# One order of side work for another in a fused attention and two-MLP kernel: where a weight's split, the steps of three batches' attention and a few late casts stand

## The chip, the cores and the metric

The kernel runs on one core of one Trainium2 chip. The metric is the device time of one execution in microseconds (us), the median of a few runs.

## The reference

Three computations follow each other. Inputs are drawn in float64 for the weights; the result is float32.

```python
x = attention(q, k, v)            # 4 batches, 8 heads, 576 tokens, 64 dims
                                  # heads 0-3: a window of 32; heads 4-7: every 32nd token
x = x.transpose(0, 2, 1, 3).reshape(2304, 512)
x = ((x @ w_a) * (x @ w_b)) @ w_out      # 512 -> 1536 -> 512
h = x @ w_in                             # 512 -> 2048
x = (h * (1 / (1 + exp(-h)))) @ w_out2   # 2048 -> 512
```

## The kernel before

**Numbers.** Every matmul operand is split in two: a high part, cast on ScalarE (ACT), and a low part, the difference, on VectorE (DVE). TensorE (PE) multiplies high by high, high by low and low by high: three passes. A weight arrives as pairs of int32 words of a float64 and has to be made float32 first, in five steps: ACT makes the exponent's rest (merge step 0, L670) and a rebased copy of the high word (L652), DVE joins them in two steps (merge 1, L673, then merge 2, L678, which reads what merge 1 wrote), and GpSimd's queue (POOL) stores the result in DRAM for later groups (L691). Then `split_w` makes the two parts, ACT's cast L698 and DVE's subtraction L699, two blocks ahead of the matmuls that use them.

**Order.** Tokens go through in five groups of 512 (the last has 256). Groups 0 and 1 run through the gated MLP (phases A0, blocks 0 to 35, and A1, 36 to 71) and the second MLP (B0, 72 to 103, and B1, 104 to 135). A block is 12 matmuls of PE, an "up" product (L706) or a "down" product (L1381 in phase A, L1401 in phase B), 2.72 us at full clock. Everything else is written by hand into the blocks: after a block's matmuls have been issued, `block(p)` runs the steps of one of two strings, the first for p below 36, the second from there on. Its letters are: 0, 1, 2 the merge steps; B the rebased copy; Y the split of the weight for block p+2; K the store to DRAM; W the loads; N, R, M, X, O a batch's attention: normalise (DVE L490, L497, POOL L503), prepare (DVE transposes L277 of q and k, scaled copies L387), mask and maximum (DVE L455, L464), softmax (ACT, one exp a segment, L478), and store of the attention's result as x (ACT L591, DVE L594). Nothing is reordered afterwards: each engine does its list in this order. Merges stand in every block from 3 to 32, and in two of three blocks from 34 to 89.

**Attention in blocks.** Batch 0 is done ahead of block 0; batches 1 to 3 are spread over the blocks by `PLAN`, which gives the block at which the batch's loads and transposes begin, the first block of each of four groups of units (two, three, two and two units), and the end of the next batch's loads. `plan_attention` sets the rest at fixed distances: scores (PE L441) at the end of block first+1, masks and exps one unit a block from first+2, normalise one block later, the transposes of probabilities (PE L523) and products with v (PE L563) later, and the store. A group's scores go into a bank of PSUM (`att`, two buffers), and the next user of the bank waits until the store has read it. Within a batch the units of the first two groups are of local heads (type 0), the other groups strided (type 1). Transposes of q and k stand one a block: of type 0 in the four blocks from the batch's start, of type 1 in four blocks that end in front of the third group.

**End of phase A.** In blocks 35 and 71 the accumulators of the gated MLP are taken out as the split y (ACT L1391, DVE L1392), which the second MLP's blocks read.

**Late stage.** From about 491 us to the end groups 2 and 3 go through as sums of seven products (up products L986, down products L1047), group 4 between them. ACT copies a product's result to `u` (L997), a DVE step joins them (L1001), then silu (ACT L1027, DVE L1029) and the split of its result (ACT L716, DVE L717). Here the order is written by the time that a table of 2.72 us per block gives each event (`ready`): the split is put where its event is due.

Of the kernel before, what the change touches and what calls it, by code (L numbers as in the profile page):

```python
# [85 lines left out]
MM, MM_HALF, BLOCK = 0.2267, 0.12, 2.72  # L86
# [8 lines left out]

PLAN = {
    1: (0, [2, 10, 19, 27], 36),
    2: (37, [41, 49, 58, 66], 79),
    3: (80, [82, 89, 97, 105], 0),
}  # L100

TOGETHER = ((0, 1), (2, 3, 4), (5, 6), (7, 8))

PAIR_OF = (2, 3)

STEPS = ("NRM0BK1O2YXW", "N0O1B2MKWYRX")

NEG = -1.0e9
REBASE = 2.0 ** -112
# [4 lines left out]
def attention_gated_mlp_silu_mlp(  # L114
# [610 lines left out]
    def plan_attention(batch, s0, first, end):  # L725

        add = lambda at, place, f, *a: plan.setdefault((at, place), []).append((f, a))

        def spread(loads, n, s0, s1):
            for m in range(n):  # L730
                add(s0 + m * (s1 - s0) // n, "load", next, loads, None)

        starts = {us[0]: s for us, s in zip(TOGETHER, first)}
        first1 = starts[NL]
        turn1 = first1 - 2
        for one in range(4):
            add(s0 + (one if batch.b > 1 else one // 2), "prepare", batch.transpose_qk, 0, one)
            add(turn1 - 4 + one, "prepare", batch.transpose_qk, 1, one)
        spread(batch.load_qk(1), 9, s0 + (4 if batch.b > 1 else 2), turn1 - 7)
        spread(batch.load_vs(), 4 * TAKE + 5, s0 + 4 * (batch.b > 1), first1 + 3)  # L740
        for us, s in zip(TOGETHER, first):
            others = len(us) - 1
            add(s + 2, "tensor", batch.scores, *us)
            for n, u in enumerate(us):
                add(s + n - others, "prepare", batch.prepare, u)
                add(s + n + 2, "mask", batch.mask, u)
                add(s + n + 2, "mask", batch.largest, u)
                add(s + n + 2, "softmax", batch.softmax, u)
                add(s + n + 3, "normalise", batch.guard, u)
                add(s + n + 3, "normalise", batch.normalise, u)  # L750
                add(s + others + 6, "turned", batch.turned, u)
                add(s + others + 7, "store", batch.store, u)
            add(s + others + 6, "tensor", batch.turn, *us)
            add(s + others + 7, "tensor", batch.values, *us)
        after = Batch(batch.b + 1, False)
        if after.b < B:
            spread(after.load_qk(0), 9, turn1 + 2, end)
            spread(after.load_vl(), 10, first1 + 7, end)
        return after
# [6 lines left out]
    def block(p):  # L766
# [5 lines left out]
        c = conv_at.get(p)  # L772
        for step in STEPS[p >= NA]:
            if step == "K":
# [16 lines left out]
    with tc.manual_schedule():  # L791
# [11 lines left out]
        batch = Batch(0, 7)  # L803
# [39 lines left out]
        for s in range(-1, max(nu + LV, max(PART), max(CONV) + 1) + 1):  # L843
# [7 lines left out]
            for step in ORDER:  # L851
# [13 lines left out]
                elif step == "A" and s in PART:  # L865
                    i = PART[s]
# [17 lines left out]
        batch = after  # L884
# [10 lines left out]
        def at(t, f, *a):  # L895
            events.append((t, len(events), f, a))
# [7 lines left out]
        def products(f, n, cost, ws=(), h=None):  # L904

            t = clock[0]
            at(t, f)
            clock[0] = t + n * cost
            for key in ws:
                used.setdefault(key, [t, t])[1] = clock[0]  # L910
            if h is not None:
                held.setdefault(h, [t, t, None])[1] = clock[0]
            return clock[0]
# [121 lines left out]
        ready = {}  # L1035
# [15 lines left out]
        def twin(n, kinds, js, half_n, fillers, places):  # L1051

            chains = [Chain(n, kind, j, c) for c, (kind, j) in enumerate(zip(kinds, js))]
            fillers = list(fillers)
            m = 0
            for s in CHAIN_ORDER:
                for chain in chains:
                    end = products(lambda s=s, chain=chain: chain.multiply(s), 6, MM, [chain.key(s)])
                    at(end, chain.evacuate, s)
                    quad = QUADS.get(s)  # L1060
                    if quad is not None and (chain.c or chain.kind == "i"):
                        j = chain.j + half_n * quad[1]
                        f, a = (gated, (chains, quad)) if chain.kind == "b" else (silu, (chain, quad))
                        if quad[0]:
                            at(end, f, *a, j)
                        else:
                            key = (chain.kind, 2, j)
                            at(end, keep_act, key, f, *a, None)
                            ready[key] = end
                    m += 1  # L1070
                    for _ in range(places.get(m, 0)):
                        if fillers:
                            products(*fillers.pop(0))
            for filler in fillers:
                products(*filler)
# [34 lines left out]
        for f in range(H1):  # L1110
            twin(("o", f), "ab", (f, f), H1, down_o(f - 1) if f else (), {10: 2})
# [14 lines left out]
        for j in range(N1):  # L1126
            key = ("b", 3, j)
# [85 lines left out]
        for f in range(0, H2, 2):  # L1213
            if f:
                twin(("p", f), "ii", (f, f + 1), H2, down_p(f - 2 + H2) + down_p(f), dict.fromkeys(range(1, 15), 1))
            else:
                last_o = [down_of("o", "b", N1 - 1, d, N1) for d in range(CC)]
                twin(("p", f), "ii", (f, f + 1), H2, last_o + down_p(f), {1: CC, **dict.fromkeys(range(9, 15), 1)})
# [4 lines left out]
        for j in range(N2):  # L1223
            key = ("i", 3, j)
# [70 lines left out]
        for key in in_order:  # L1295
# [4 lines left out]
            elif key[0] == "B":  # L1300
                n, c = key[1:]
                kind, j = ("ab"[c], n[1]) if n[0] == "o" else ("i", n[1] + c)
                needs((kind, j), (n, c, 0), t)
            elif key[0] == "B22":
                for c in range(2):
                    n = key[1]
                    kind, j = ("ab"[c], n[1] + H1) if n[0] == "o" else ("i", n[1] + c + H2)
                    needs((kind, j), (n, c, 1), t)
            elif key[0] == "T12":
                n, c = key[1:]  # L1310
# [30 lines left out]
        for ph, g in PHASES:  # L1341
# [7 lines left out]
            for kind, j in half[ph]:  # L1349
                if batch.b < B and p == PLAN[batch.b][0]:  # L1350
                    batch = plan_attention(batch, *PLAN[batch.b])
# [111 lines left out]
```

## Time and profile before

| | us |
|---|---|
| median of 3 runs (lowest to highest) | 944.64 (941.54 to 947.15) |
| the profiled execution | 944.54 |
| span of its trace | 942.7 |
| PE busy in it | 920.4 (98%) |
| DVE busy | 665.6 (71%) |
| ACT busy | 541.3 (57%) |
| POOL busy | 82.3 (9%) |
| mean granted clock of PE | 0.989 |

The span is the traced part of the execution; 1.8 us lie around it. PE is busy nearly throughout, so what can be won is the time in which it stands still, and the time in which it works at the lower clock. The waits of PE by cause, and the stretch in which they lie, are the views to read; the other engines' busy shares are means over stages that differ.

### The profile page before, as it was taken

What the parts mean: (1) busy time and instruction counts of PE and PEld (TensorE: products, weight loads), DVE (VectorE), ACT (ScalarE), POOL (GpSimd) and SP (SyncE); (2) the same over time, 40 slices, a digit from 0 to 9 for tenths busy, and PEclk for the clock granted to TensorE, in tenths of its full rate; (3) what the DMA queues carried; (4) which work ended last, traced back from release to release, by engine and by line L of the source; (5) the groups of instructions that cost most, each with busy time, mean ns of one, the idle gap of its engine ahead of it and who ended that gap; (6) DMA issues with size and microseconds to landing.
All of it is one profiled execution on the core that took longest, in us unless ns stands there. A gap on an engine that the chain in (4) does not pass through costs nothing.

```text
span 942.7 us, 15848 instructions
## 1 busy us (share of the span) xinstructions
PE 920.4 (98%) x5626; PEld 748.3 (79%) x5626; DVE 665.6 (71%) x1248; ACT 541.3 (57%) x1274; POOL 82.3 (9%) x139
## 2 busy tenths in 40 slices
PE   9999899999999989999999999999999999999998
PEld 5767678787778778778888888888999788878897
DVE  5588888776777767666777666665587776766475
ACT  3558778666667566565543444345575554554474
POOL 2232222111111111100000000000000000000000
PEclk9799999999999999999999999999999999999999
DMA  9999789898888995333242222223464121225361
GB/s 168 196 280 276 230 250 277 255 241 251 254 232 237 272 219 179 108 86 97 92 116 75 67 67 67 57 72 120 123 184 141 45 83 58 83 67 168 119 207 45
DMA packets 163647, 145.29 MB, mean 154 GB/s; under 512 B 96800, under 2 KB 119904, under 8 KB 163568
## 3 DMA queue, kind: packets, MB, share of 16 engines
q1 hardware_dynamic: 154758, 121.81, 48.1%
q0 software_dynamic: 6720, 21.63, 6.9%
q10 hardware_dynamic: 2090, 0.84, 0.4%
q8 instruction: 44, 0.72, 0.3%
q14 instruction: 35, 0.29, 0.1%
HBM read 121.70 MB, written 22.54 MB: 153 GB/s over the span
## 4 chain that ended last, share of the span: by engine, by line
PE 71%; DVE 12%; ACT 7%; issue 4%; DMA 4%; POOL 0%; SPq 0%; DVEq 0%; ACTq 0%; POOLq 0%
PE ring L706 15%; PE ring L986 12%; PE att L986 8%; PE acc L1047 8%; PE acc L1401 6%; PE acc L1173 4%; PE att L1047 4%; PE ring L1047 4%; PE acc L706 3%; ACT prs L478 2%; DVE raw L673 2%; DVE raw L678 2%; DVE w L699 2%; PE acc L1381 1%; ACT raw L670 1%
## 5 line engine op out<-in xcount | busy, mean ns | idle before, releaser
L706 PE MATMUL ring<-x,w 128*128 128x512 f32 (+1 forms) x816 | 168.3, 358 | 6.7 <-DVE w L699 5.6
L706 PEld LDWEIGHTS ring<-x,w 128*128 128x128 f32 x816 | 133.6, 191 | 33.3 <-DVE w L699 10.2
L1277 DVE TENSOR_TENSOR w<-raw,w 128x512 fp32r<-128x512 f32 (+1 forms) x164 | 106.2, 655 | 29.5 <-ACT w L1276 26.7
L1276 ACT CAST w<-raw 128x512 fp32r<-128x512 f32 (+1 forms) x164 | 95.7, 592 | 20.8 <-PE att L1047 11.0
L699 DVE TENSOR_TENSOR w<-raw,w 128x512 fp32r<-128x512 f32 x136 | 93.1, 692 | 3.7 <-ACT w L698 2.7
L706 PE MATMUL ring<-y,w 128*128 128x512 f32 x384 | 94.0, 394 | 0.0
L1401 PE MATMUL acc<-w,h 128*128 128x512 f32 x384 | 93.3, 392 | 0.6 <-DVE w L699 0.4
L698 ACT CAST w<-raw 128x512 fp32r<-128x512 f32 x136 | 82.5, 619 | 4.0 <-DVE raw L678 4.0
L1401 PEld LDWEIGHTS acc<-w,h 128*128 128x128 f32 x384 | 71.3, 188 | 17.0 <-DVE w L699 1.6
L706 PEld LDWEIGHTS ring<-y,w 128*128 128x128 f32 x384 | 71.8, 189 | 15.6 <-DVE w L699 0.6
L716 ACT CAST h<-h 128x512 fp32r<-128x512 f32 (+1 forms) x48 | 27.2, 567 | 86.8 <-DVE h L1022 41.0
L1381 PE MATMUL acc<-h,w 128*128 128x512 f32 x288 | 72.2, 397 | 3.5 <-DVE w L699 2.0
L1381 PEld LDWEIGHTS acc<-h,w 128*128 128x128 f32 x288 | 52.8, 188 | 18.1 <-DVE w L699 4.0
L717 DVE TENSOR_TENSOR h<-g,h 128x512 fp32r<-128x512 f32 (+1 forms) x64 | 39.9, 624 | 31.6 <-ACT h L716 31.4
L986 PE MATMUL ring<-operands,w 128*128 128x512 f32 x240 | 61.3, 398 | 0.0
L716 ACT CAST h<-g 128x512 fp32r<-128x512 f32 (+1 forms) x64 | 36.3, 567 | 42.4 <-DVE g L1373 30.4
L986 PE MATMUL ring<-x,w 128*128 128x512 f32 x240 | 59.5, 391 | 1.2 <-ACT u L997 1.2
L986 PE MATMUL att<-operands,w 128*128 128x512 f32 x240 | 60.4, 395 | 0.0
L478 ACT ACTIVATE prs<-sm,nm 128x54 f32<-128x54 f32 (+1 forms) x120 | 39.7, 333 | 30.0 <-DVE nm L464 29.7
L673 DVE SCALAR_TENSOR_TENSOR raw<-words,raw 128x512 int32<-128x512 int32 x68 | 47.7, 702 | 10.7 <-ACT raw L670 10.0
L986 PEld LDWEIGHTS ring<-operands,w 128*128 128x128 f32 x240 | 44.9, 188 | 11.7 <-DVE w L1277 1.1
L678 DVE SCALAR_TENSOR_TENSOR raw<-e,raw 128x512 int32<-128x512 int32 x68 | 48.8, 718 | 7.5 <-ACT e L652 0.7
(200 smaller groups left out, 1559.8 us busy)
## 6 DMA issues: line engine op xcount, KB each, us to landing
raw<-keptp SPq DMA_DIRECT2D x80, 256.0 KB
raw<-kepti SPq DMA_DIRECT2D x64, 256.0 KB
words<-in_moe_w_out_dram SPq DMA_DIRECT2D x28, 512.0 KB
raw<-kepto SPq DMA_DIRECT2D x48, 256.0 KB
raw<-kepta SPq DMA_DIRECT2D x36, 256.0 KB
raw<-keptb SPq DMA_DIRECT2D x36, 256.0 KB
words<-in_moe_w_in_dram SPq DMA_DIRECT2D x16, 512.0 KB
words<-in_moe_w_a_dram SPq DMA_DIRECT2D x12, 512.0 KB
```

Source lines behind the costliest of these rows:

```text
L673: nc.vector.scalar_tensor_tensor(out=z, in0=high, scalar=SIGN, in1=z, op0=ALU.bitwise_and, op1=ALU.bitwise_or)
L678: nc.vector.scalar_tensor_tensor(out=z, in0=rebased.pop(c), scalar=3, in1=z, op0=ALU.logical_shift_left, op1=ALU.bitwise_or)
L698: nc.scalar.copy(out=o[:, 0], in_=t)
L699: nc.vector.tensor_tensor(out=o[:, 1], in0=t, in1=o[:, 0].bitcast(F32), op=ALU.subtract)
L706: nc.tensor.matmul(ps[:, :T], lhsT=w[:, wi, c * P:(c + 1) * P], rhs=x[:, xi, c, :T], start=(c == 0 and wi == 0 and xi == 0), stop=(c == CC ...
L716: nc.scalar.copy(out=o[:, 0, :T], in_=t32[:, :T])
L986: nc.tensor.matmul(self.acc[acc], lhsT=w[:, wi, (2 * part + c) * P:(2 * part + c + 1) * P], rhs=x[:, xi, c], start=(begin and c == 0 and m ...
L1047: nc.tensor.matmul(accs[d], lhsT=lhsT, rhs=rhs, start=(first and wi == 0 and xi == 0), stop=(last and wi == 1))
L1276: nc.scalar.copy(out=o[:, 0, cols], in_=t)
L1277: nc.vector.tensor_tensor(out=o[:, 1, cols], in0=t, in1=o[:, 0, cols].bitcast(F32), op=ALU.subtract)
L1381: nc.tensor.matmul(accs[d], lhsT=w[:, wi, d * P:(d + 1) * P], rhs=h[:, xi], start=(j == 0 and wi == 0 and xi == 0), stop=(j == N1 - 1 and ...
L1401: nc.tensor.matmul(accs[t][:, :DM], lhsT=h[:, xi, t * P:(t + 1) * P], rhs=w[:, wi, :], start=(j == 0 and wi == 0 and xi == 0), stop=(j == ...
```

## The change

It consists of five edits. In the strings the split Y goes between merge 1 and merge 2 (on ACT ahead of B; from block 36 on also ahead of the mask M). Batches 2 and 3 get other first blocks in `PLAN`, and batch 3's start and the loads' ends move with them. The type-1 transposes stand one block later relative to their group. In `plan_attention` a unit's store is put a block later for the third unit of a group of three. In the late stage the split of the second MLP's silus made from the chain's product 2 is due one block later (16 such events).

```diff
--- before.py
+++ after.py
@@ -95,15 +95,15 @@
 
 PLAN = {
     1: (0, [2, 10, 19, 27], 36),
-    2: (37, [41, 49, 58, 66], 79),
-    3: (80, [82, 89, 97, 105], 0),
+    2: (37, [41, 49, 59, 68], 76),
+    3: (76, [79, 87, 97, 105], 0),
 }
 
 TOGETHER = ((0, 1), (2, 3, 4), (5, 6), (7, 8))
 
 PAIR_OF = (2, 3)
 
-STEPS = ("NRM0BK1O2YXW", "N0O1B2MKWYRX")
+STEPS = ("NRM0K1YBO2XW", "N0O1YB2MKWRX")
 
 NEG = -1.0e9
 REBASE = 2.0 ** -112
@@ -732,7 +732,7 @@
 
         starts = {us[0]: s for us, s in zip(TOGETHER, first)}
         first1 = starts[NL]
-        turn1 = first1 - 2
+        turn1 = first1 - 1
         for one in range(4):
             add(s0 + (one if batch.b > 1 else one // 2), "prepare", batch.transpose_qk, 0, one)
             add(turn1 - 4 + one, "prepare", batch.transpose_qk, 1, one)
@@ -749,7 +749,7 @@
                 add(s + n + 3, "normalise", batch.guard, u)
                 add(s + n + 3, "normalise", batch.normalise, u)
                 add(s + others + 6, "turned", batch.turned, u)
-                add(s + others + 7, "store", batch.store, u)
+                add(s + others + 7 + n // 2, "store", batch.store, u)
             add(s + others + 6, "tensor", batch.turn, *us)
             add(s + others + 7, "tensor", batch.values, *us)
         after = Batch(batch.b + 1, False)
@@ -1066,7 +1066,7 @@
                         else:
                             key = (chain.kind, 2, j)
                             at(end, keep_act, key, f, *a, None)
-                            ready[key] = end
+                            ready[key] = end + BLOCK * (chain.kind == "i" and s == 2)
                     m += 1
                     for _ in range(places.get(m, 0)):
                         if fillers:
```

On ACT, around block 20 of phase A0: `L591 COPY` is the store of the third unit of a group, which frees its PSUM bank (L1364 is the copy of a gate's product). Before:

```order
L670 ACTIVATE raw<-words 128x512
L652 ACTIVATE e<-words 128x512
L591 CAST x<-att 128x2x128
L591 CAST x<-att 128x2x64
L591 COPY x<-att 128x2x64 x2
L698 CAST w<-raw 128x512
L670 ACTIVATE raw<-words 128x512
L652 ACTIVATE e<-words 128x512
L698 CAST w<-raw 128x512
L1364 COPY a<-ring 128x512
```

After:

```order
L670 ACTIVATE raw<-words 128x512
L698 CAST w<-raw 128x512
L652 ACTIVATE e<-words 128x512
L591 CAST x<-att 128x2x128
L591 CAST x<-att 128x2x64
L591 COPY x<-att 128x2x64
L670 ACTIVATE raw<-words 128x512
L698 CAST w<-raw 128x512
L652 ACTIVATE e<-words 128x512
L591 COPY x<-att 128x2x64
L1364 COPY a<-ring 128x512
```

The third unit's copy moves behind the next block's three instructions (L670, L698, L652), and L698 goes ahead of L652 in each block.

On DVE, in blocks 70 and 71, at the end of phase A1 (L1392 is the low part of y). Before:

```order
L490 TENSOR_SCALAR su<-su 128x4
L497 RECIPROCAL rs<-su 128x4
L673 SCALAR_TENSOR_TENSOR raw<-words,raw 128x512
L678 SCALAR_TENSOR_TENSOR raw<-e,raw 128x512
L699 TENSOR_TENSOR w<-raw,w 128x512
L1392 TENSOR_TENSOR y<-acc_2299,y 128x512
L1392 TENSOR_TENSOR y<-acc_2300,y 128x512
L1392 TENSOR_TENSOR y<-acc_2301,y 128x512
L1392 TENSOR_TENSOR y<-acc_2302,y 128x512
L673 SCALAR_TENSOR_TENSOR raw<-words,raw 128x512
L678 SCALAR_TENSOR_TENSOR raw<-e,raw 128x512
```

After:

```order
L673 SCALAR_TENSOR_TENSOR raw<-words,raw 128x512
L699 TENSOR_TENSOR w<-raw,w 128x512
L678 SCALAR_TENSOR_TENSOR raw<-e,raw 128x512
L455 SCALAR_TENSOR_TENSOR sm<-att,mask_str 128x162 x2
L464 TENSOR_REDUCE nm<-sm 128x6
L1392 TENSOR_TENSOR y<-acc_2299,y 128x512
L1392 TENSOR_TENSOR y<-acc_2300,y 128x512
L1392 TENSOR_TENSOR y<-acc_2301,y 128x512
L1392 TENSOR_TENSOR y<-acc_2302,y 128x512
L490 TENSOR_SCALAR su<-su 128x6
L497 RECIPROCAL rs<-su 128x6
L673 SCALAR_TENSOR_TENSOR raw<-words,raw 128x512
```

A unit's mask and maximum (L455, L464) now stand ahead of y's evacuation, the guard and reciprocal (L490, L497) behind it, and each split L699 between L673 and L678.

On DVE, the last transposes of batch 3's first k (`kT`, before in blocks 82 and 83, now in 78 and 79). Before:

```order
L699 TENSOR_TENSOR w<-raw,w 128x512
L277 STREAM_TRANSPOSE kT<-kld 128x576
L1373 SCALAR_TENSOR_TENSOR g_4005<-th,ring 128x512
L717 TENSOR_TENSOR h<-g_4005,h 128x512
L699 TENSOR_TENSOR w<-raw,w 128x512
L277 STREAM_TRANSPOSE kT<-kld 128x576
L673 SCALAR_TENSOR_TENSOR raw<-words,raw 128x512
L678 SCALAR_TENSOR_TENSOR raw<-e,raw 128x512
L455 SCALAR_TENSOR_TENSOR sm<-att,mask_loc 128x128 x2
L464 TENSOR_REDUCE nm<-sm 128x4
```

After:

```order
L673 SCALAR_TENSOR_TENSOR raw<-words,raw 128x512
L699 TENSOR_TENSOR w<-raw,w 128x512
L678 SCALAR_TENSOR_TENSOR raw<-e,raw 128x512
L277 STREAM_TRANSPOSE kT<-kld 128x576
L673 SCALAR_TENSOR_TENSOR raw<-words,raw 128x512
L699 TENSOR_TENSOR w<-raw,w 128x512
L678 SCALAR_TENSOR_TENSOR raw<-e,raw 128x512
L1373 SCALAR_TENSOR_TENSOR g_3994<-th,ring 128x512
L717 TENSOR_TENSOR h<-g_3994,h 128x512
L699 TENSOR_TENSOR w<-raw,w 128x512
L455 SCALAR_TENSOR_TENSOR sm<-att,mask_loc 128x128 x2
L464 TENSOR_REDUCE nm<-sm 128x4
```

Before, the last transpose had two instructions between it and the first mask of those keys; now a merge with its split, a silu's two steps (L1373, L717) and another split stand between them.

## Rows read from the trace of the kernel before

**Rows 1.** Page, section 4: chain of waits that ended last, by engine

```profile
PE 71%; DVE 12%; ACT 7%; issue 4%; DMA 4%; POOL 0%; SPq 0%; DVEq 0%; ACTq 0%; POOLq 0%
```

**Rows 2.** Table by stretch: length, busy us per engine, PEclk, DMA share

```profile
56.00:178.00 122.00, 113.79 (x826) 88.79 (x824) 102.48 (x198) 90.80 (x234) 24.18 (x41) 0.99 0.96 262
...
178.00:293.00 115.00, 111.62 (x792) 88.35 (x793) 83.99 (x166) 75.77 (x203) 18.81 (x29) 1.00 0.87 246
...
293.00:436.00 143.00, 138.70 (x984) 112.10 (x983) 98.86 (x194) 88.17 (x232) 15.17 (x24) 0.99 0.62 173
```

**Rows 3.** Waits of PE, whole span: us in total, times, longest

```profile
PE ring L706 <- DVE w L699: 5.6, 7, 2.0
PE att L441 <- DVE kT L277: 5.1, 4, 2.9
PE acc L1381 <- DVE w L699: 2.0, 2, 1.4
PE ring L986 <- ACT u L997: 1.2, 1, 1.2
PE ring L706 <- ACT x L591: 1.0, 1, 1.0
```

**Rows 4.** Timeline, DVE in phase A0: start, us, engine, line, operation

```profile
92.20 0.69 DVE L673 SCALAR_TENSOR_TENSOR raw<-words,raw 128x512 int32<-128x512 int32 x1
...
92.99 0.69 DVE L678 SCALAR_TENSOR_TENSOR raw<-e,raw 128x512 int32<-128x512 int32 x1
...
93.60 0.69 DVE L699 TENSOR_TENSOR w<-raw,w 128x512 fp32r<-128x512 f32 x1
...
94.20 0.48 DVE L455 SCALAR_TENSOR_TENSOR sm<-att,mask_loc 128x128 f32<-128x128 f32 x2
...
95.06 0.68 DVE L673 SCALAR_TENSOR_TENSOR raw<-words,raw 128x512 int32<-128x512 int32 x1
```

**Rows 5.** Timeline around the end of block 20, ACT and PE

```profile
124.51 0.72 PE L441 MATMUL att<-kT,qs 64*64 64x54 f32 x20
124.64 0.74 ACT L670 ACTIVATE raw<-words 128x512 int32<-128x512 uint8 x1
```

**Rows 6.** Page, section 5: two groups of ACT, busy us, mean ns

```profile
L698 ACT CAST w<-raw 128x512 fp32r<-128x512 f32 x136 | 82.5, 619 | 4.0 <-DVE raw L678 4.0
...
L478 ACT ACTIVATE prs<-sm,nm 128x54 f32<-128x54 f32 (+1 forms) x120 | 39.7, 333 | 30.0 <-DVE nm L464 29.7
```

**Rows 7.** Timeline of the phase's end: evacuation of y, then the next matmuls

```profile
291.41 2.63 ACT L1391 CAST y<-acc 128x512 fp32r<-128x512 f32 x4 [0.42 <-PE acc L1381]
...
292.57 2.47 DVE L1392 TENSOR_TENSOR y<-acc,y 128x512 fp32r<-128x512 f32 x4
...
296.44 2.77 PE L706 MATMUL ring<-y,w 128*128 128x512 f32 x10
```

**Rows 8.** Timeline of the scores of batch 3's first group, DVE and PE

```profile
328.38 0.77 DVE L277 STREAM_TRANSPOSE kT<-kld 128x576 f32<-128x576 f32 x1
...
329.30 0.27 PE L441 MATMUL att<-kT,qT 64*32 64x64 f32 x2 [0.87 <-DVE kT L277]
...
331.62 0.77 DVE L277 STREAM_TRANSPOSE kT<-kld 128x576 f32<-128x576 f32 x1
...
332.44 1.96 PE L441 MATMUL att<-kT,qT 64*32 64x64 f32 x62 [2.88 <-DVE kT L277]
```

**Rows 9.** Table by stretch, as Rows 2, just after three waits of PE

```profile
103.40:107.40 4.00, 3.97 (x10) 3.16 (x11) 3.64 (x11) 3.24 (x10) 1.14 (x2) 0.57 0.70 210
...
236.60:239.00 2.40, 2.40 (x11) 1.98 (x12) 2.02 (x5) 1.17 (x4) 0.97 (x2) 1.00 0.92 351
...
332.40:336.00 3.60, 3.56 (x67) 3.11 (x68) 2.76 (x6) 0.66 (x4) 0.00 (x0) 0.55 0.96 191
```

**Rows 10.** Timeline, DVE idle behind a softmax of batch 3

```profile
391.60 0.69 DVE L1373 SCALAR_TENSOR_TENSOR g<-th,ring 128x512 f32<-128x512 f32 x1 [2.06 <-ACT th L1371]
```

**Rows 11.** Timeline, PE's longest wait for a split

```profile
103.43 2.85 PE L706 MATMUL ring<-x,w 128*128 128x512 f32 x6 [2.00 <-DVE w L699]
```

## The prediction, on record before the changed kernel ran

> **What bounds the kernel now.** I read first the chain of waits that ended last: the tensor engine (PE) holds 71% of it, VectorE (DVE) 12%, ScalarE (ACT) 7% [rows 1]. So time is won or lost where PE waits for one of those two, and nowhere else. Then the table by stretch says where it waits: PE stands idle 8.2 us of the 122 in phase A0, 3.4 of 115 in A1 and 4.3 of 143 in the phases B [rows 2]. DVE is busy for 102 of the first 122 us, against 84 of 115 and 99 of 143 afterwards: it sets the pace in A0, while later it has slack that is not evenly spread. Last, the waits of PE by cause [rows 3]: 5.6 us in seven waits for a weight's low part, 5.1 for the transposed keys, 2.0 in two waits for a low part in the down products, 1.2 for a copied `u` in the late stage, 1.0 for a stored x. These are what the change can take away; behind a long wait PE also works at a lower clock for some us (below).
>
> The sum is made against the profiled execution, 944.54 us, which is 0.1 under the median of the three runs. About 0.5%, 4.7 us, is what a measurement of this kernel can tell from no change.
>
> **The change, part by part.**
>
> *The split between the merges, phase A0.* Merge 2 reads what merge 1 wrote, and starts 0.79 us after it (92.20 to 92.99); the split behind it belongs to another weight and starts 0.61 after merge 2 [rows 4]. With the split between them all three can start 0.61 apart, so a block with a merge is 0.18 shorter on DVE. Up to block 20 that is 18 merges, 3.2 us at most, but there the moved store takes it back (next paragraph). From block 21 to 34 there are 13 merges: 13 x 0.18 = 2.3. I take **-2.3**; the bounds are 0 (DVE waits for ACT's merge step 0 in place of the old gap) and -5.2 (all 29 merges of blocks 3 to 32, without a toll at block 20).
>
> The Trainium skill, page "VectorE: DVE Perf Modes", section "The DRAIN you can't avoid", speaks against this term: the next DVE operation starts only when the pipe is empty, and "you cannot skip it by chaining ops without semaphores"; the section itself sends instructions that nothing holds to another section, where they may start earlier. By the first sentence the order of the three would not matter and the term would be 0. The rows do not agree with it: the two starts are 0.79 and 0.61 apart, the second less than the 0.69 that the instruction itself takes [rows 4].
>
> *The third unit's store a block later.* At block 20 the second scores product takes a PSUM bank when the third unit's copy has read it. Before, PE starts there at 124.51, and block 20's first ACT instruction follows at 124.64 [rows 5]. Now three of those (an exponent step, a cast, a rebased copy, each about 0.62 as the cast's mean [rows 6]) stand ahead of the copy: 3 x 0.62 = 1.9 us. PE comes to it that much too early, and the 3.2 us of the first 20 blocks end there. From block 36 on the same move has no scores close behind it. So nothing is added beyond the lost gain.
>
> *Block 36.* PE waits 1.0 us for x, which ACT stores at the change of phase [rows 3]. ACT's cast for the split now goes ahead of the store: 0.62 [rows 6]. **+0.6** (0 to +0.7).
>
> *Batch 2, blocks 41 to 66.* Masks now stand behind a split, 0.61 later, and the type-1 transposes and the last two groups one or two blocks later. The two waits in the down products, 2.0 together, lie here [rows 3]: they may shorten by 1.4 or grow by 0.61 each. **+0.4** (-1.4 to +1.2), near no change, since the number of operations is the same.
>
> *Blocks 70 and 71.* A mask with its six exps is put into block 70, in front of y's evacuation. The exps are 0.33 each, 2.0 together [rows 6]. Before, ACT began y's casts at 291.41, as the accumulators ended, and DVE ended the low parts at 292.57 + 2.47 = 295.04 [rows 7]. Now both are 2.0 later, 297.0, and behind them stand a guard, a reciprocal, a merge and the split for block 73, some 1.5 us: 298.5. PE wants it at 296.44 [rows 7], so it waits 2.1 there and up to 1.0 in block 74, whose split follows. **+2.6** (+2.0 to +3.1).
>
> *Keys of batch 3.* The last two transposes came 0.87 and 2.88 us too late, 3.75 together, and the scores and the block behind them ran at 0.55 of the clock for 3.6 us, which loses 1.6 [rows 8, 9]: 5.4. Now the last transpose stands a whole block, 2.72 us, further ahead of the scores. PE was there 0.87 + 0.27 + 2.88 = 4.0 before the last one was done, so 4.0 - 2.72 = 1.3 could be left; DVE's list in these blocks is a little shorter, so I take 0.7, too short a wait for the clock to fall. **-4.7** (-5.4 to -4.1).
>
> *Masks of batch 3.* Its groups begin three and two blocks earlier, where merges still run. A mask and its maximum take 0.86 (94.20 to 95.06 [rows 4]). The nearest row is a block that has a transpose beside its split: DVE went round in 3.24 us (328.38 to 331.62 [rows 8]) against PE's 2.72, so it loses 0.5 a block; with a mask as well 1.4. The first group has two such blocks, 81 and 82: +2.8 less what lead the splits have there; **+2.4** (+1.4 to +3.4, the last with the split's 0.61). Of the second group one mask falls on the last merge, block 89: 0 to 0.86 + 0.79 + 0.61 = 2.3, **+1.2**. In the last two groups masks stand 0.61 later, behind a split. DVE idles 2.06 us behind such a softmax [rows 10] because its next list waits for ACT, so a later mask is passed on: up to 0.61 for each of four units, 2.4; half of it, **+1.2**, since the splits have about that lead. Together +4.8.
>
> *Late silus.* The split's ACT cast goes behind the copy of `u` that PE waits 1.2 us for [rows 3]. **-1.2** (-1.2 to 0); the other fifteen casts have no wait of PE near them, and cost nothing while a block's lead remains.
>
> Sum: -2.3 + 0.6 + 0.4 + 2.6 - 4.7 + 4.8 - 1.2 = +0.2, so 944.54 + 0.2 = **944.7 us**.
>
> **The rivals.**
>
> *Slower: three new waits reach 2 us and the clock falls.* After a wait of 2.00 us the clock stood at 0.57 for 4.0 us, which costs 4.0 x 0.43 = 1.7 on top [rows 9, 11]; after one of 1.4 (the longest in the down products [rows 3]) it stayed at 1.00 [rows 9]. My sum puts waits of about that size at blocks 73 and 85 and a shorter one at 103. Where each comes out as one piece of 2.0 or more, it adds 3 x 1.7 = 5.1: 949.8. For it: the estimates at 73 and 85 are above 2. Against it: a loss can come as several short waits.
>
> *Faster: the splits' lead covers the masks.* DVE is idle 31 us of 115 in A1 and 44 of 143 in B [rows 2], and the number of masks is what it was. If the splits stand two blocks ahead by enough, the terms +2.6 and +4.8 are gone: 937.3. Against it: DVE already was late before at just such places, 5.6 and 2.0 us [rows 3].
>
> *The exchange of the merges gives nothing.* If the gap of 0.79 only moves, the term -2.3 is missing: 947.0.
>
> **How the numbers follow.** The forecast, waits removed about as large as waits made, has 0.40; the faster rival 0.30, since seven of its us rest on leads that I worked out by hand and not on a row; the slower one 0.21; the exchange without gain 0.09. Faster by over 0.5% is under 939.8: the faster rival and a little of the forecast's lower side, less the part of that rival that stops short, 0.32. Slower is above 949.3: the slower rival with some of the upper bounds, 0.22. The rest, 0.46, lies between. The range goes from 936, just below the faster rival, to 951.5, above the slower one by 1.7, one more fall of the clock.
>
> **What would show it.** In the changed profile: DVE's merge 1, split and merge 2 at 0.61 us steps; no wait for a low part between blocks 21 and 35, but one of some 2 us before the second scores product at block 20; the wait of the scores for keys under 1 us; a wait for the low part at blocks 73 and 85 of about 2 us each, and short ones at 103 and 111; no wait for `u` in the late stage. Wrong would be the whole account if PE's idle time fell in A0 by 5 us, or if no wait for a split appeared between 290 and 350 us; and the sum, if a clock of 0.55 showed behind more than one of them.

## The result, and the profile after

The changed kernel takes 955.93 us, the median of four runs (952.51 to 958.27); the kernel before beside it 944.86. The ratio is 1.0117 (1.0073 to 1.0161): **slower by 11 us**. The forecast was 944.7, with no change as the likeliest and 951.5 as the upper end. The profiled execution of the changed kernel is its shortest, 952.51, with a span of 950.7.

From 33 to 45 us of the profiled execution before, PE works at 0.50 of its clock; after, at 1.00. Both happen in executions of the other kernels below too, so the two traces are compared from block 5 on, by the start of each block's first matmul.

| start of | before | after | difference | since the row above |
|---|---|---|---|---|
| block 5 | 68.16 | 66.05 | -2.1 | |
| block 16 | 107.41 | 101.30 | -6.1 | -4.0 |
| block 23 | 131.47 | 132.31 | +0.8 | +7.0 |
| block 36 | 175.48 | 173.74 | -1.7 | -2.6 |
| block 72 | 293.25 | 293.57 | +0.3 | +2.1 |
| block 77 | 309.19 | 314.21 | +5.0 | +4.7 |
| block 84 | 334.33 | 335.05 | +0.7 | -4.3 |
| block 116 | 436.74 | 446.09 | +9.4 | +8.6 |
| end of the span | 942.7 | 950.7 | +8.0 | -1.4 |

The first row is that difference of the start. From block 5 on the change loses 8.0 + 2.1 = 10.1 us, near the 11.1 of the medians. The table by stretch of the changed kernel (length, busy us of PE, PEld, DVE, ACT, POOL, then PE's clock) answers to [rows 2]:

```profile
56.00:178.00 122.00, 112.17 (x815) 89.09 (x813) 99.32 (x199) 91.53 (x234) 23.17 (x40) 0.96 0.95 267
178.00:293.00 115.00, 111.10 (x790) 87.85 (x791) 80.14 (x155) 70.94 (x184) 16.29 (x26) 1.00 0.88 243
293.00:436.00 143.00, 133.48 (x912) 104.70 (x911) 96.34 (x193) 87.21 (x237) 19.41 (x27) 0.98 0.63 167
```

PE's idle time in the third stretch is now 143 - 133.5 = 9.5 us, where it was 4.3. The waits of PE over the span (total, times, longest) answer to [rows 3]:

```profile
PE acc L1401 <- ACT w L698: 5.2, 4, 2.7
PE ring L706 <- ACT w L698: 3.4, 4, 1.8
PE ring L706 <- DVE w L699: 2.4, 3, 1.4
PE att L441 <- DVE x L594: 2.3, 2, 1.4
PE att L441 <- DVE kT L277: 2.1, 3, 1.5
PE ring L706 <- ACT x L591: 1.9, 1, 1.9
PE att L441 <- ACT x L591: 1.5, 1, 1.5
PE acc L1401 <- DVE w L699: 1.4, 3, 0.5
```

The waits for a split's low part on DVE have shrunk, those for keys fell from 5.1 to 2.1 (1.9 of it at block 3), and the wait for `u` is gone. In their place stand waits for the split's **high** part, ACT's cast L698, 8.6 us in all, and waits for x at blocks 11 and 20, where a PSUM bank has to come free. Before, PE waited for the cast once:

```profile
PE acc L1381 <- ACT w L698: 0.6, 1, 0.6
```

The waits of ACT between 178 and 436 us, before and then after, tell why the casts are late:

```profile
ACT prs L478 <- DVE nm L464: 26.6, 18, 2.9
```

```profile
ACT prs L478 <- DVE nm L464: 37.6, 18, 3.0
```

ACT waits for a unit's maximum 18 times in both, once for each unit of batches 2 and 3, and 11.0 us longer: 0.61 a unit on average, near the 0.60 after which the next instruction starts behind a split. In the change single units differ from before by -0.9 to +2.7, since the plan moves them too; where only the mask goes behind the split (below), 16 of the 18 wait 0.36 to 0.78 longer.

Blocks 99 to 101 have no merge and the same group of units in both kernels, so they show it closest. The timeline (start, duration, engine, line) of ACT and DVE before:

```profile
383.53 0.62 ACT L698 CAST w<-raw 128x512 fp32r<-128x512 f32 x1
385.44 0.34 ACT L478 ACTIVATE prs<-sm,nm 128x54 f32<-128x54 f32 x1 [1.29 <-DVE nm L464]
387.39 0.61 ACT L698 CAST w<-raw 128x512 fp32r<-128x512 f32 x1
```

```profile
384.27 0.55 DVE L455 SCALAR_TENSOR_TENSOR sm<-att,mask_str 128x162 f32<-128x162 f32 x2
384.85 0.49 DVE L464 TENSOR_REDUCE nm<-sm 128x6 f32<-128x324 f32 x1
385.26 0.68 DVE L699 TENSOR_TENSOR w<-raw,w 128x512 fp32r<-128x512 f32 x1
```

And after:

```profile
390.25 0.62 ACT L698 CAST w<-raw 128x512 fp32r<-128x512 f32 x1
392.76 0.34 ACT L478 ACTIVATE prs<-sm,nm 128x54 f32<-128x54 f32 x1 [1.90 <-DVE nm L464]
394.72 0.60 ACT L698 CAST w<-raw 128x512 fp32r<-128x512 f32 x1
```

```profile
390.98 0.69 DVE L699 TENSOR_TENSOR w<-raw,w 128x512 fp32r<-128x512 f32 x1
391.58 0.56 DVE L455 SCALAR_TENSOR_TENSOR sm<-att,mask_str 128x162 f32<-128x162 f32 x2
392.17 0.49 DVE L464 TENSOR_REDUCE nm<-sm 128x6 f32<-128x324 f32 x1
394.84 0.17 DVE L490 TENSOR_SCALAR su<-su 128x6 f32<-128x6 f32 x1 [2.18 <-ACT prs L478]
...
395.36 0.69 DVE L699 TENSOR_TENSOR w<-raw,w 128x512 fp32r<-128x512 f32 x1
```

Before, from ACT's cast to its next cast: 3.86 us (383.53 to 387.39). DVE makes mask and maximum meanwhile, ACT makes six exps, and DVE's split lies beside the exps. After: 4.47 us (390.25 to 394.72). The two engines work as **a ring**: DVE's split needs ACT's cast of the same block, the mask now stands behind the split, the exps need the maximum, and the next cast stands behind the exps. DVE closes it on its side too: the guard of the sums (L490) waits 2.18 us for the exps, and the next split and mask stand behind it. Everything in the ring lengthens the round, here by 0.61 us; the split, which lay outside it, is now inside. PE's blocks are 2.72, so the lead of the splits melts until PE waits for a cast, here at the start of block 103, where before it did not wait:

```profile
401.61 0.73 PE L1401 MATMUL acc<-w,h 128*128 128x512 f32 x2 [0.85 <-ACT w L698]
```

Two more places. At the end of block 20, timeline of PE and the third unit's copy on ACT:

```profile
121.22 0.35 PE L441 MATMUL att<-kT,qs 64*64 64x54 f32 x2 [1.36 <-DVE x L594]
...
122.80 0.25 ACT L591 COPY x<-att 128x128 f32<-128x128 f32 x1
...
123.11 1.54 PE L441 MATMUL att<-kT,qs 64*64 64x54 f32 x46 [1.53 <-ACT x L591]
```

PE waits there twice, 1.36 and 1.53, and the clock is 0.50 in the 4 us behind it (first row of the next fence). And at y's evacuation, ACT, DVE, POOL and PE:

```profile
293.82 2.01 ACT L1391 CAST y<-acc 128x512 fp32r<-128x512 f32 x4
294.42 2.48 DVE L1392 TENSOR_TENSOR y<-acc,y 128x512 fp32r<-128x512 f32 x4 [2.65 <-ACT y L1391]
...
297.45 1.05 POOL L503 TENSOR_TENSOR prs<-prs,rs 128x324 f32<-128x324 f32 x1 [13.11 <-ACT e L652]
297.82 1.22 DVE L699 TENSOR_TENSOR w<-raw,w 128x512 fp32r<-128x512 f32 x1
...
299.10 3.97 PE L706 MATMUL ring<-y,w 128*128 128x512 f32 x10 [1.41 <-DVE w L699]
```

It begins at 293.82 in place of 291.41, as the forecast had it. The split for block 73 then takes 1.22 us in place of 0.69, beside a normalisation on POOL. With a wait of 0.50 for a cast ahead of these rows and one of 0.73 behind them, in block 74, PE waits 2.6 us there. The table by stretch just behind the waits of blocks 20, 73, 85 (2.67 us) and 103 (PE's clock is the sixth figure behind the length, the counts in brackets left out, as in the first table):

```profile
124.60:128.60 4.00, 4.00 (x13) 3.13 (x11) 2.85 (x6) 2.67 (x14) 0.00 (x0) 0.50 0.68 212
299.10:303.10 4.00, 3.97 (x10) 2.61 (x10) 2.28 (x8) 2.40 (x10) 0.52 (x1) 0.61 0.84 262
340.70:344.70 4.00, 3.86 (x10) 2.57 (x11) 3.81 (x8) 2.09 (x5) 1.82 (x3) 0.57 0.95 169
401.60:404.00 2.40, 1.93 (x7) 1.38 (x8) 2.30 (x6) 1.00 (x2) 1.03 (x1) 1.00 0.19 23
```

### The profile page after: what moved, and what is told of

Read it like the earlier page. It is cut to its first block, busy times and chain, and to the rows that moved or that the text cites. A ratio compares the mean times of both kernels' runs of the same rounds, so it can differ in the third digit from the quotient of the medians.

```text
span 950.7 us, 15841 instructions
## 1 busy us (share of the span) xinstructions
PE 921.7 (97%) x5626; PEld 748.5 (79%) x5626; DVE 662.4 (70%) x1248; ACT 540.2 (57%) x1274; POOL 83.9 (9%) x139
## 4 chain that ended last, share of the span: by engine, by line
PE 68%; DVE 11%; ACT 9%; DMA 6%; issue 5%; SPq 1%; POOL 0%; DVEq 0%; ACTq 0%; POOLq 0%
PE ring L706 14%; PE ring L986 12%; PE att L986 9%; PE acc L1047 8%; PE acc L1401 6%; PE acc L1173 4%; PE att L1047 4%; PE ring L1047 4%; ACT prs L478 3%; PE acc L706 2%; DVE raw L678 2%; DVE w L699 1%; DVE raw L673 1%; PE acc L801 1%; ACT h L716 1%
## 5 line engine op out<-in xcount | busy, mean ns | idle before, releaser
L699 DVE TENSOR_TENSOR w<-raw,w 128x512 fp32r<-128x512 f32 x136 | 97.3, 718 | 8.8 <-ACT w L698 7.3
L1401 PE MATMUL acc<-w,h 128*128 128x512 f32 x384 | 96.1, 399 | 6.7 <-ACT w L698 5.2
L698 ACT CAST w<-raw 128x512 fp32r<-128x512 f32 x136 | 82.9, 618 | 5.3 <-DVE raw L678 5.3
L717 DVE TENSOR_TENSOR h<-g,h 128x512 fp32r<-128x512 f32 (+1 forms) x64 | 39.9, 624 | 28.9 <-ACT h L716 28.9
L673 DVE SCALAR_TENSOR_TENSOR raw<-words,raw 128x512 int32<-128x512 int32 x68 | 48.0, 706 | 13.7 <-ACT raw L670 10.8
L986 PEld LDWEIGHTS att<-operands,w 128*128 128x128 f32 x240 | 45.1, 188 | 10.9
```

What stands on the lines that cost most here:

```text
L673: nc.vector.scalar_tensor_tensor(out=z, in0=high, scalar=SIGN, in1=z, op0=ALU.bitwise_and, op1=ALU.bitwise_or)
L698: nc.scalar.copy(out=o[:, 0], in_=t)
L699: nc.vector.tensor_tensor(out=o[:, 1], in0=t, in1=o[:, 0].bitcast(F32), op=ALU.subtract)
L986: nc.tensor.matmul(self.acc[acc], lhsT=w[:, wi, (2 * part + c) * P:(2 * part + c + 1) * P], rhs=x[:, xi, c], start=(begin and c == 0 and m ...
L1401: nc.tensor.matmul(accs[t][:, :DM], lhsT=h[:, xi, t * P:(t + 1) * P], rhs=w[:, wi, :], start=(j == 0 and wi == 0 and xi == 0), stop=(j == ...
```

## The experiments

Medians of several runs of each, with the ratio to the kernel before, run beside them on the same chip; its medians in the four groups of runs were 943.92, 944.59, 942.53 and 943.48. Where a string or a number isn't named, it is that of the kernel before.

### The parts of the change, each alone

The strings:

```diff
-STEPS = ("NRM0BK1O2YXW", "N0O1B2MKWYRX")
+STEPS = ("NRM0K1YBO2XW", "N0O1YB2MKWRX")
```

> The strings alone. Theory A (the dear part is that masks and softmaxes of batches 2 and 3 now stand at the phase's end and among merges): the strings by themselves gain in phase A0 (the wait of 2.0 at block 15 and those at 24, 25, 33 go, about -6) and give back about 1.2 at block 11 and 1.4 at block 20, where the split now stands ahead of the store that frees a PSUM bank, and 0.6 to 1.2 at block 36; after block 36 about +1. Sum about -2 to -4, so 941 to 943. Theory B (the dear part is the split ahead of mask, store and rebased copy): +5 or more, 950 and above.

Measured: 951.57, ratio 1.0072 (1.0050 to 1.0095). Theory A is wrong here and B right. In its trace blocks 5 to 36 gain about 2 us, and from there on it loses: at blocks 46, 64, 71, 84, 95, 102, 103, 110 and 111 (each with the wait that ends it), between 0.5 and 1.6 us at a place.

The plan of batches 2 and 3, and the type-1 transposes:

```diff
-    2: (37, [41, 49, 58, 66], 79),
-    3: (80, [82, 89, 97, 105], 0),
+    2: (37, [41, 49, 59, 68], 76),
+    3: (76, [79, 87, 97, 105], 0),
...
-        turn1 = first1 - 2
+        turn1 = first1 - 1
```

> The plan of batches 2 and 3 and the later type-1 transposes alone. Theory A: the scores' wait for the keys goes (-4.5), the evacuation of y behind six exps costs 4 to 5 between blocks 72 and 77, the masks in blocks 81 to 94 cost 5 to 6; sum +5 to +6, so about 950. Theory B: the losses come only with the split ahead of the mask; -4 to -2, so 941 to 943.

Measured: 947.34, ratio 1.0039 (1.0022 to 1.0056). Between the two theories, nearer to A and with its signs: from block 77 to 84 it gains 4.2 us, but blocks 72 to 77 lose 6.1, and blocks 84 to 116 4.5, of which 3.0 at blocks 92 to 94.

The third unit's store:

```diff
-                add(s + others + 7, "store", batch.store, u)
+                add(s + others + 7 + n // 2, "store", batch.store, u)
```

> The third unit's store a block later, alone. Theory A and B alike: the second scores product at block 20 waits for ACT's copy behind the next block's instructions, 1.5 to 2 us, and the clock may fall behind it (1 to 2 more); elsewhere nothing. +2 to +4, so 946.5 to 948.5. A rival (the copy is not what holds the bank): no change.

Measured: 947.79, ratio 1.0028 (1.0011 to 1.0045), as expected in size. But part of it lies at a place that I had not seen: with batch 3's groups where they were, the scores at the end of block 98 wait 2.74 us for the same store.

```profile
386.35 1.47 PE L441 MATMUL att<-kT,qs 64*64 64x54 f32 x46 [2.74 <-DVE x L594]
```

In the full change the group before it starts two blocks earlier, and this wait isn't there.

The late silus' splits:

```diff
-                            ready[key] = end
+                            ready[key] = end + BLOCK * (chain.kind == "i" and s == 2)
```

> The late silus' splits a block later, alone: PE's wait for the copied u (1.2 us) goes and nothing else moves; -1.3, so about 943.3. A rival (the block's delay makes another event late): a wait of PE for the split of a silu appears in the late stage, 0 to +1.

Measured: 941.47, ratio 0.9976 (0.9956 to 0.9995). The wait for `u` is gone from its list, and no wait came for it in the late stage; from block 116 to the end its trace is 1.4 us shorter.

By the ratios the strings cost 6.8, the plan 3.7 and the store 2.6 us, and the silus give 2.3: 10.8 together, near the change's 11. That they add up so well is in part luck, for the store's wait at block 98 isn't in the change.

### What in the strings costs

The first string alone:

```diff
-STEPS = ("NRM0BK1O2YXW", "N0O1B2MKWYRX")
+STEPS = ("NRM0K1YBO2XW", "N0O1B2MKWYRX")
```

> The first string as in the change (blocks 0 to 35), the second as before. Theory A (the second string holds the loss of the strings): phase A0 gains the 2.0 wait of block 15 and those of 24 and 33 and gives back 1.2 at block 11 and 1.4 at block 20, so -2 to -3, about 941.5, and after block 36 every block is as before. Rival B (a faster A0 only moves DVE's lateness on, or the waits for the PSUM bank eat all of it): 0 to +2.

Measured: 943.93, ratio 0.9987 (0.9970 to 1.0003). Between the two: the long wait of block 15 is gone, and waits of 1.4 at block 11, 1.1 at block 20 and a longer one at block 36 have come. So the loss of the strings, 8 us of difference to the run with both, is the second one's.

The split between the merges in the first string, but behind the store and in ACT's old order:

```diff
-STEPS = ("NRM0BK1O2YXW", "N0O1B2MKWYRX")
+STEPS = ("NRM0BK1OY2XW", "N0O1B2MKWYRX")
```

> The first string with the split between the merges, but behind the store as before (store, split, merge 2), and on ACT in the order of before; second string as before. Theory A (the exchange gains 0.18 a merge on DVE, and its toll comes only from the split's place ahead of the store): no wait at blocks 11 and 20, the gain of A0 whole: -4 to -6, about 939. Rival B (the exchange does not help DVE, what A0 gained came from ACT's earlier cast): within 1 us of before, 943 to 945, and merge 2 not closer to merge 1.

Measured: 944.87, ratio 1.0003 (0.9989 to 1.0018). Rival B's time. DVE's three steps stand 0.6 us apart in some merges, as in the first three of these lines, and not in others (start, duration, engine, line):

```profile
111.36 0.65 DVE L673 SCALAR_TENSOR_TENSOR raw<-words,raw 128x512 int32<-128x512 int32 x1
111.93 0.68 DVE L699 TENSOR_TENSOR w<-raw,w 128x512 fp32r<-128x512 f32 x1
112.53 0.68 DVE L678 SCALAR_TENSOR_TENSOR raw<-e,raw 128x512 int32<-128x512 int32 x1
...
117.04 0.69 DVE L673 SCALAR_TENSOR_TENSOR raw<-words,raw 128x512 int32<-128x512 int32 x1 [1.45 <-ACT raw L670]
118.12 0.69 DVE L699 TENSOR_TENSOR w<-raw,w 128x512 fp32r<-128x512 f32 x1 [0.39 <-ACT w L698]
```

Here DVE waits for ACT, 1.45 us for merge step 0 and 0.39 for the cast. Of 27 merges ahead of block 36 whose split follows merge 1, it starts 0.77 us behind at the median, where the whole change has 0.60: with ACT's cast behind the rebased copy, the gap has only moved. DVE's wait for the cast between 64 and 176 us, which the list of the kernel before does not have:

```profile
DVE w L699 <- ACT w L698: 4.5, 13, 0.7
```

The waits at blocks 11 and 20 are here too (0.66 and 1.03 us), though the store is where it was. So they don't come from the split's place ahead of the store alone; what else makes the store late for PE is not shown.

The mask ahead of the split and of merge 2:

```diff
-STEPS = ("NRM0BK1O2YXW", "N0O1B2MKWYRX")
+STEPS = ("NRM0BK1O2YXW", "N0O1MYB2KWRX")
```

> The first string as before; the second with the split between the merges but the mask ahead of it (mask, split, rebased copy, merge 2), so that only the mask's place differs from the change. Theory A (the loss of the second string comes from masks, and so exps, that start one split later): most of the +7 to +9 is gone, -1 to +1, about 943.5. Rival B (it comes from the split's own place, ACT's cast ahead of the rebased copy and DVE's ahead of merge 2): +4 or more, as with the change's string, 948 and above.

Measured: 938.96, ratio 0.9943 (0.9921 to 0.9964). Better than theory A said: **the same split between the merges, with the mask ahead of it, comes with a gain of 5.6 us and no loss.** Which of the two moves brings the gain, the next run tells. PE has no wait for a weight left between 180 and 290 us. ACT's wait for the maxima, between 178 and 436 us:

```profile
ACT prs L478 <- DVE nm L464: 21.0, 18, 2.5
```

Only the mask moved forward, the split left in its old place:

```diff
-STEPS = ("NRM0BK1O2YXW", "N0O1B2MKWYRX")
+STEPS = ("NRM0BK1O2YXW", "N0O1MB2KWYRX")
```

> The kernel before with only the mask moved ahead of merge 2 in the second string; the split stays behind the store to DRAM, where it was. Theory A (the mask's place is what counts, 0.6 to 0.8 us earlier for each unit): -4 to -5, 940. Rival B (it was the split's own place between the merges that gained there): 944 to 946.

Measured: 938.81, ratio 0.9959 (0.9940 to 0.9978). So most or all of that gain is the mask's place, not the split's. ACT's wait for the maxima is 21.6 us here, nearly the same. In both traces the gain lies between blocks 36 and 72 (5.2 and 3.9 us); from 84 to 116 they differ from before by 0.4 and 0.1.

Only the mask moved behind the split:

```diff
-STEPS = ("NRM0BK1O2YXW", "N0O1B2MKWYRX")
+STEPS = ("NRM0BK1O2YXW", "N0O1B2YMKWRX")
```

> The kernel before, and in the second string only the mask moved behind the split (merge 1, merge 2, split, mask): no split between the merges. Theory A (the place of the mask against the split is by itself the loss of the change's second string): +6 to +9, 949 to 952, with waits of PE for ACT's cast at blocks 102 and 110 as in the change. Rival B (the loss needs the split between the merges, whose cast then goes ahead of the rebased copy): 0 to +3.

Measured: 953.11, ratio 1.0110 (1.0075 to 1.0146), a little above theory A's range. One mask behind one split, nothing else, costs as much as the whole change. In its trace PE, ACT and POOL run their instructions in the order of before, and only DVE's order differs. Splits that run longer than 0.70 us beside POOL (the effect shown at the end) are not the cause: there are three here, five before and eleven in the change. ACT's wait for the maxima is that of the change, and PE waits for casts ahead of blocks 47, 55, 57, 64, 103 and 111:

```profile
ACT prs L478 <- DVE nm L464: 37.6, 18, 2.9
...
PE acc L1381 <- ACT w L698: 2.1, 2, 1.5
PE acc L1401 <- ACT w L698: 2.0, 2, 1.1
PE ring L706 <- ACT w L698: 1.2, 2, 0.6
```

The whole change with the mask ahead:

```diff
-STEPS = ("NRM0K1YBO2XW", "N0O1YB2MKWRX")
+STEPS = ("NRM0K1YBO2XW", "N0O1MYB2KWRX")
```

> The whole change, but in its second string the mask ahead of the split (mask, split, rebased copy, merge 2). Theory A (a mask's place in a block is passed on by the exps to ACT's casts and so to the splits, nearly once for each of 18 units): the change's loss of 11 becomes about 11 - 13 = -2, so 941 to 945. Rival B (the gain of the mask ahead exists only with the plan of before, whose masks stand elsewhere): 950 and above.

Measured: 937.37, ratio 0.9940 (0.9916 to 0.9963). The letter M, moved ahead of Y, B and 2, turns a change that loses 1.2% into one that gains 0.6%. Between blocks 84 and 116 its trace loses 1.8 us to the one before, where the change's loses 8.6.

### What in the plan costs

Only batch 3's transposes a block earlier:

```diff
-    2: (37, [41, 49, 58, 66], 79),
-    3: (80, [82, 89, 97, 105], 0),
+    2: (37, [41, 49, 58, 66], 78),
+    3: (79, [82, 89, 97, 105], 0),
```

> Of the plan only this: batch 3's transposes begin one block earlier (and the loads for them end one earlier), all groups of batches 2 and 3 stay where they were. Theory A (the gain of the plan is the scores' wait for the keys, and its loss is the places of the masks and of y's evacuation): the 3.7 us of waits at block 83 with the clock behind them fall to about 1, nothing else changes; -4 to -4.5, about 939.7. Rival B (that wait gave DVE the time to get ahead, and its loss reappears as waits for splits at blocks 84 to 97): -1 to +1.

Measured: 941.02, ratio 0.9967 (0.9954 to 0.9980). Block 83 is 4.4 us shorter; 1.2 of it comes back at block 87, where PE waits 0.7 for a split.

The whole change, without a mask ahead of y's evacuation:

```diff
-    2: (37, [41, 49, 59, 68], 76),
+    2: (37, [41, 49, 58, 66], 76),
```

> The whole change, but batch 2's third and fourth group begin at blocks 58 and 66 as before, so that no mask with six exps stands ahead of y's evacuation in block 70. Theory A: the waits at blocks 72 to 75, about 5 us with the clock behind them, go: 950 to 952. Rival B (those blocks are late from the splits' place alone): 955 to 957.

Measured: 948.75, ratio 1.0085 (1.0055 to 1.0115), against 1.0117 (1.0073 to 1.0161) of the change. The intervals overlap, so it is the trace that decides for theory A: blocks 72 to 77 lose nothing, where the change's lose 4.7. The six exps ahead of y thus cost some 3 to 5 us of the change's 11; the wait for a cast at block 85, 2.8 us, is still there (the longest of this row):

```profile
PE acc L1401 <- ACT w L698: 5.3, 4, 2.8
```

### Faster than both

```diff
-    2: (37, [41, 49, 58, 66], 79),
-    3: (80, [82, 89, 97, 105], 0),
+    2: (37, [41, 49, 58, 66], 78),
+    3: (79, [82, 89, 97, 105], 0),
...
-STEPS = ("NRM0BK1O2YXW", "N0O1B2MKWYRX")
+STEPS = ("NRM0BK1O2YXW", "N0O1MYB2KWRX")
...
-                            ready[key] = end
+                            ready[key] = end + BLOCK * (chain.kind == "i" and s == 2)
```

> Three parts together on the kernel before: second string with the mask first, then the split between the merges (-5.6 alone), batch 3's transposes a block earlier (-3.6 alone), the late silus' splits a block later (-2.4 alone). Theory A: they lie in different stages and add up, -11 to -12, so 932 to 934. Rival B: the ground won by the first is what the second needs, -6 to -8, 937 to 938.

Measured: 932.82, ratio 0.9900 (0.9870 to 0.9930). That is theory A's time, but 9.7 us under the 942.53 beside it, where the three alone sum to 11.6: they add up for the most part, within the interval.

With the change's batch 3 and its type-1 transposes in place of the shift by one block (the edit is against the run above):

```diff
-    2: (37, [41, 49, 58, 66], 78),
-    3: (79, [82, 89, 97, 105], 0),
+    2: (37, [41, 49, 58, 66], 76),
+    3: (76, [79, 87, 97, 105], 0),
...
-        turn1 = first1 - 2
+        turn1 = first1 - 1
```

> The kernel before with the second string that puts the mask first, then the split between the merges; batch 3's plan of the change (groups from 79 and 87), batch 2's groups as before, the type-1 transposes and the late silus' splits a block later; first string and store as before. Theory A (the plan's loss was y's evacuation and the masks behind splits, both gone here, and the scores' wait for the keys is gone): 930 to 934. Rival B (batch 3's early masks among merges cost 3 or more whatever the string): 935 to 938.

Measured: 933.24, ratio 0.9889 (0.9861 to 0.9916), the same within the intervals. So batch 3's early groups lose little by themselves, once masks stand ahead. The table by stretch of both, the run above and then this one (PE's busy time is the first figure behind the length):

```profile
178.00:293.00 115.00, 114.88 (x839) 93.28 (x840) 85.99 (x172) 80.66 (x211) 19.10 (x30) 1.00 0.91 258
293.00:436.00 143.00, 141.90 (x990) 114.74 (x986) 99.45 (x196) 87.93 (x231) 14.65 (x23) 1.00 0.59 168
```

```profile
178.00:293.00 115.00, 114.88 (x842) 93.40 (x842) 86.19 (x172) 80.64 (x211) 19.23 (x30) 1.00 0.94 257
293.00:436.00 143.00, 140.73 (x982) 113.56 (x979) 98.92 (x195) 87.12 (x229) 14.98 (x23) 1.00 0.60 166
```

PE's idle time falls from 3.4 and 4.3 us [rows 2] to 0.1 and 1.1 in the first, 0.1 and 2.3 in the second: about 1 us is what the early groups cost.

## Why the prediction was wrong

The forecast's terms and the trace, by stretch: blocks 5 to 36, -2.3 and +0.4; 36 to 72, +1.0 and +2.1; 72 to 77, +2.6 and +4.7; 77 to 84, -4.7 and -4.3; 84 to 116, +4.8 and +8.6; the rest, -1.2 and -1.4. So the miss is spread over four of them: 2.7, 1.1, 2.1 and 3.8. The mask's place alone, ahead of the split and of merge 2, takes the whole change from a ratio of 1.0117 to 0.9940, more than the whole miss.

- *What bounds the kernel.* Right as far as it went: PE waits for DVE and ACT. But I took DVE alone as the pace and read ACT as its supplier. The row of the exps stood among my own rows, with "30.0 <-DVE nm L464 29.7" at its end [rows 6]: ACT idles 30 us for maxima. I used only its duration. That idle time was the sign that ACT's list is closed by DVE's mask in every block with a unit.
- *Masks behind a split: the step that failed.* For batch 2 I put +0.4, "near no change, since the number of operations is the same", and 1.2 for the last two groups of batch 3, "half of it". The runs show 0.61 for each of 18 units, 11.0 us of ACT's wait, and the mask alone behind the split measures 1.0110 (1.0075 to 1.0146), some 10 us. The mechanism, a later mask passed on by the exps, was written down, but for four units out of 18, and as something that a lead would absorb. In a ring each round is longer, and a lead only puts the wait off.
- *The exchange of merge 2 and split, A0.* The size of DVE's gain was right where ACT's cast goes first (0.60 us steps in the change), the end wrong. For the first string alone, with no moved store, my terms come to -5.2 and +0.6, so -4.6; it measures -0.7 (ratio 0.9987, 0.9970 to 1.0003). The pure exchange measures nothing, much as the bound of 0 had it: DVE waits for ACT in place of the gap, for the cast more than for merge step 0. So the rival without that gain was right in this step, though 9 us short in its sum. The rule that I weighed against the term, from the Trainium skill's page "VectorE: DVE Perf Modes", section "The DRAIN you can't avoid", is not the reason: the three starts closed up to 0.57 and 0.60 us where ACT's cast was there.
- *The store at block 20.* "Nothing is added beyond the lost gain" was wrong: PE waits 1.36 and 1.53 us there, and the clock is 0.50 in the 4 us behind. To block 16 the change gains 4.0 and from there to 23 loses 7.0, so 3.0 are added. The clock fell behind the two waits, though neither was 2 us.
- *Block 36.* +0.6 forecast; the wait there grew from 1.0 to 1.9.
- *y's evacuation.* The mechanism was right (casts at 293.8, and 293.4 is what 2.0 us later comes to), and so was the size of the waits: +2.6 forecast, 0.50 + 1.41 + 0.73 = 2.6 seen. But blocks 72 to 77 lose 4.7, for behind the waits the clock is 0.61 for 4.0 us, which costs 1.6. In the whole change with the mask ahead, whose clock is 1.00 there (296 to 300), the same exps ahead of y cost 1.9.
- *Keys.* -4.7 forecast, -4.3 between blocks 77 and 84. *Late silus.* -1.2 forecast, -1.4 in the trace.
- *Masks of batch 3 among merges.* +4.8 forecast for blocks 81 to 111, +8.6 seen from 84 to 116. The cause is not the merges alone: the plan by itself loses 4.5 there with the string of before, 8.6 with the change's, and 1.8 with the mask ahead.
- *The rivals.* The slower one had its places right, blocks 73, 85 and 103, though at 85 and 103 PE waits for ACT's cast and not for the low part, and the clock did fall at two of them (0.61 and 0.57), not behind the 0.85 at 103 (1.00). A clock near 0.55 behind more than one wait was the sign named for a wrong sum, and it came at blocks 20, 73 and 85. But this rival said 949.8, 6 short, for it priced only what I had already found; none of the rivals asked what a place in the string is worth in all 18 units.

The mask alone behind the split loses only 6.1 us from block 5 on in its trace, where the medians say 9.6. Its profiled execution, 951.88, is the shortest of its four, and the one before, 944.54, is 1.1 above the median beside it, so these two differ by 7.3, of which 1.3 lie ahead of block 5. Inside, it loses 7.8 and wins 1.8 back from block 77 to 84, where behind the wait for the keys its clock is 1.00 (337.1 to 340.7) and was 0.55 before [rows 9]. So 6 to 10 us is what these runs say of the price.

## What to carry to other kernels

Where two engines hand work back and forth once in every block, look for the ring, and ask of every moved step whether it goes into the ring or out of it; its price is up to its own length times the number of rounds (here 11.0 us of ACT's wait, and 6 to 10 us of time), and no mean busy share shows it. The idle time at the end of a row, with the name of what ended it, points to the ring. Of two orders with the same work, the one that serves the engine which hands work back first wins: the mask before the split; by the medians 4 to 6 us were won here by moving it forward, and 10 lost by moving it back.

## What the runs showed of the hardware

- A low part of 128x512 on DVE (L699) took 0.69 us alone and 1.22 beside a normalisation on POOL (297.45 to 298.50). Over the 16 traces it depends on which starts first: of the 2176 splits none of the 1909 without a normalisation (L503) beside them took longer than 0.70, nor any of the 110 that started before it, but 107 of the 157 that started after it, up to 1.23. The kernel before has five of these, the changed one eleven.
- The clock also fell behind two shorter waits in a row: 0.50 after 1.36 and 1.53 at block 20. Behind a wait of 0.85 at block 103 it stayed at 1.00.
- One and the same wait did not always bring the fall, so a fixed price for a wait of 2 us, as in the prediction, is not borne out. Behind 2.00 us at block 15 the clock was 0.57 before [rows 9] and 1.00 in the run with the mask behind the split (104.65 to 108.65). Behind 1.13 and 0.45 us at block 111 it was 1.00 in the changed kernel (429.5 to 433.5), and behind 1.14 and 0.45 there 0.60 with the strings alone (425.3 to 429.3).
- A fall did not always cost time either: blocks 5 to 36 took 107.3 us before, with the fall at block 15, and 107.3 in the run with the mask behind the split, which has none there.
